# First tiles of pooled attention: which engine sums which piece of k and v, where the gate products stand, and q of the second block in two transfers

## The chip, the core and the metric

The kernel runs on one core of a Trainium2 chip. A core has five engines, each with its own instruction queue: TensorE (PE in the profile, with PEld for its weight loads), VectorE (DVE), ScalarE (ACT), GpSimd (POOL) and SyncE (SP, which here only issues transfers). They meet through semaphores. PE writes its products to PSUM; DVE and ACT read PSUM and SBUF, and POOL works on SBUF. The metric is the device time of one execution in microseconds, the median of several runs.

## The reference, cut to what matters

Eight batches of eight heads with 576 queries each. k and v are averaged over groups of eight rows, so 72 keys are left per head; attention over them is followed by a mixture of eight experts whose routing depends on all tokens.

```python
k_p = k.reshape(B, H, Sp, pool, D).mean(axis=3)
v_p = v.reshape(B, H, Sp, pool, D).mean(axis=3)
scores = scale * np.matmul(q, k_p.transpose(0, 1, 3, 2))
scores = scores - np.max(scores, axis=-1, keepdims=True)
attn = np.exp(scores)
attn = attn / (np.sum(attn, axis=-1, keepdims=True) + 1e-09)
out = np.matmul(attn, v_p)
# x = out by token; logits = x @ w_gate; each token goes to one expert, at most N // E to each
h = np.maximum(x[mask] @ w1[e], 0.0)
out[mask] = h @ w2[e]
```

## The kernel before

**Tiles and blocks.** The 4608 tokens are worked in 36 tiles of 128. A block is one batch: its k (`rawk`, four pairs of heads, each 8 x 72 numbers a partition), its v (`rawv`, five chunks of 8 x 64) and its q (`rawq`). A block has 4.5 tiles, so tile 4 takes queries of blocks 0 and 1 and needs the sums of both. The pooled k stands in `kblk`, the pooled v with a mask in `vblk`; `vblk` also has eight columns that hold v times the gate weights, so that the attention products give the routing's logits too, and one column of ones for the sum of the weights.

**Sums of a block.** `pool_k` (L171) adds eight rows in three steps, 8 to 4 to 2 to 1 (L175, L176, and L179 twice, once for each head of a pair). `pool_v` (L181) does the same for v (L188 to L190) and then multiplies the sums by the mask into `vblk` (L198). For blocks 1 to 7 POOL does all of this, one block behind the other. For block 0 the work is shared: `pool_k` runs on DVE for three of the four pairs, `add_k` (L144) adds the last pair on PE as eight products with the unit matrix, and ACT copies the result (L152). Of v, DVE adds three chunks, `add_v` (L154) adds two on PE, ACT copies and masks these, and POOL masks DVE's.

**Gate columns.** `prep_v` (L202) transposes the sums of v on PE (L211), ACT copies them, `prep_g` (L215) multiplies them by the gate weights on PE (L220), and DVE masks them into `vblk` (L221).

**A tile.** `st_s` (L224) computes the scores into `pss`, which has one buffer. `softmax` (L236) takes the maximum (L240) and the difference (L241) on DVE, which frees `pss`, and the exponential on ACT (L242). One tile later `st_e` transposes the weights (L259) in two parts `pse` and `rt`, and ACT copies them to `eT` (L260). Two tiles later `st_av` makes the attention products into `psa` (L272), and three tiles later `norm` divides on DVE (L284 to L297) and stores.

**What sets the order.** The schedule is written out by hand in `run`: each engine works in the order in which the program emits its instructions, and the loop over tiles interleaves them. `plan` sets at which tile POOL's sums of a block and the loads of a later one are issued. `behind` puts `prep_v` directly behind the scores of the block's first full tile (tile 5 for block 1) and `prep_g` behind the next. For block 0, `prep_v` stands at tile 1's end and `prep_g` ahead of tile 2's scores. SP issues the transfers of block 0 in pieces and then k, v and q of blocks 1 and 2. Before all this PE is kept busy by 13 products of ones (`warm`, L503), and DVE makes constants for the routing (`more`, L464 on).

Of the kernel before, what the change touches and what calls it, by code (L numbers as in the profile page):

```python
# [23 lines left out]
class Attention:  # L24
# [119 lines left out]
    def add_k(self, b, j):  # L144

        nc = self.nc
        ps = self.ps0[:, 0, 384:456]
        for t in range(8):
            nc.tensor.matmul(ps, self.ident, self.rk[b][:, j, t], start=(t == 0), stop=(t == 7))
        for a in range(2):  # L150
            h, y = slice(64 * a, 64 * a + 64), slice(72 * a, 72 * a + 72)
            nc.scalar.activation(self.kblk[b % 4][h, j, y], ps[h], AF.Copy)  # L152

# [27 lines left out]
    def pool_v(self, b, eng, c=slice(0, 5), blocks=None):  # L181
# [9 lines left out]

        for m0, m1 in ((0, 1), (1, 2), (2, 5)):
            m0, m1 = max(m0, c.start), min(m1, c.stop)
            if m0 < m1:
# [3 lines left out]
                (blocks or eng).tensor_tensor(v[:, o, :64].rearrange("p (c i) d -> p c i d", c=n),  # L198
# [16 lines left out]
    def prep_g(self, b):  # L215
# [3 lines left out]
        for n, o in enumerate((slice(0, 40), slice(40, 72), slice(72, 88))):  # L219
            nc.tensor.matmul(ps[:, o], self.vT[:, n], self.wblk[:, o], start=True, stop=True)  # L220
        nc.vector.tensor_tensor(self.vblk[b % 4][:, :, 64:72], ps[:, :88].rearrange("p (n e) -> p n e", e=8),  # L221
                                self.mask[:, :, None].to_broadcast([128, 11, 8]), op=OP.mult)
# [11 lines left out]

    def softmax(self, i):
        nc = self.nc  # L236
        ps = self.pS.pop(i)[:, :, :288].rearrange("p g (h y) -> p g h y", h=4)
        mx = self.wk.tile([128, 2, 4], F32, name="mx")
        e = self.wk.tile([128, 2, 4, 72], F32, name="e", bufs=3)
        nc.vector.tensor_reduce(mx, ps, axis=AX.X, op=OP.max)  # L240
# [86 lines left out]
    def run(self, ctx, full, consts, more, after, end, warm):  # L327
# [82 lines left out]
class Routing:  # L410
# [24 lines left out]
    def consts(self, jp, ident):  # L435
# [25 lines left out]
        self.jp = jp  # L461

    def more(self):
        nc, cst, J, NC, jp = self.nc, self.cst, self.J, self.NC, self.jp  # L464
        self.tri = cst.tile([128, 128], BF, name="tri")
        nc.vector.tensor_scalar(self.tri, jp, 0.0, None, op0=OP.is_gt)
        self.untri = cst.tile([128, 128], BF, name="untri")
        nc.vector.tensor_scalar(self.untri, self.tri, -31.0, None, op0=OP.mult)

# [4 lines left out]
        self.spread = cst.tile([128, 224], F16, name="spread")  # L474
# [1043 lines left out]
```

## Time and profile before

| what | value |
|---|---|
| median of 3 runs (lowest, highest) | 602.14 us (601.81, 602.21) |
| the profiled execution | 602.19 us, its span 600.4 us |
| ACT busy over the span | 306.1 us (51%) |
| POOL busy in 20 to 100 us, by the windows view | 9.47 to 9.71 of each 10 us |
| DMA share in the same view, 10 to 70 us | 1.01 to 1.02 |
| DMA queue of SP, q1 | 70.66 MB, 35.6% of 16 engines over the span |
| granted TensorE clock | 0.984 in the mean, 0.74 in 125 to 150 us |

The page gives busy time over the whole span, which mixes attention (to about 130 us), routing (to about 155 us) and the experts. Where a change touches the first 30 us only, the timeline and the chain of work that ended last, both for that window, say more. In a row of the timeline stand the start, the busy time, the engine, the line of the program, the operation, what it writes and reads with shapes, and in brackets how long the engine was idle before it and what it waited for. In a row of the chain stand the start, the length, the engine, and the tile with the line.

### The profile page before, as it was taken

The page shows a single profiled execution, that of the slowest core. Times are in us where ns is not written, and L with a number is a line of the kernel's source. Part 1 is how long each engine was busy: PE and PEld are TensorE (multiplying, and loading weights), DVE is VectorE, ACT ScalarE, POOL GpSimd, SP SyncE. Part 2 cuts the span into 40 slices and gives each one's busy share as a digit, 9 for nine tenths or more (in the row PEclk, how much of TensorE's full clock was granted, in tenths as well). Part 3 has the DMA queues.
Part 4 walks back from the last instruction along what each step waited for, and adds up shares of the span by engine and source line. Part 5 has one row for each costly group of instructions (what it writes and reads, how often), then busy time and mean ns, then how long its engine had stood idle before and what let it go on. Part 6 is the DMA issues. An engine that isn't in the chain of part 4 may idle for free.

```text
span 600.4 us, 11097 instructions
## 1 busy us (share of the span) xinstructions
PE 576.1 (96%) x4061; PEld 510.1 (85%) x4061; DVE 396.6 (66%) x1155; ACT 306.1 (51%) x629; POOL 176.6 (29%) x219
## 2 busy tenths in 40 slices
PE   8999999995899999999999999999999999999993
PEld 5999999983798789779978987997899899889972
DVE  7677887987886778758965886496477437416200
ACT  7444444451461375385774585276449627835210
POOL 1999999100300410231132112122221211220021
PEclk9999999995999999999999999999999999999998
DMA  8999972122530862548547346543743563450010
GB/s 353 419 422 408 423 292 89 72 89 88 168 142 23 257 202 84 162 109 293 98 107 251 129 98 201 167 106 73 257 135 80 158 228 78 100 192 11 2 58 26
DMA packets 63872, 99.83 MB, mean 166 GB/s; under 512 B 34736, under 2 KB 34752, under 8 KB 61120
## 3 DMA queue, kind: packets, MB, share of 16 engines
q1 hardware_dynamic: 52560, 70.66, 35.6%
q0 software_dynamic: 5920, 18.89, 10.0%
q10 hardware_dynamic: 5328, 9.48, 4.2%
q8 instruction: 34, 0.56, 0.4%
q14 instruction: 30, 0.25, 0.1%
HBM read 72.40 MB, written 18.87 MB: 152 GB/s over the span
## 4 chain that ended last, share of the span: by engine, by line
PE 78%; issue 7%; DVE 6%; POOL 3%; DMA 3%; ACT 1%; POOLq 0%; another core or an unknown queue 0%; SPq 0%; ACTq 0%; DVEq 0%
PE h L1094 30%; PE h L1130 25%; PE psa L272 6%; PE pss L230 5%; PE h L1135 4%; PE pse L259 2%; DMA xg<-xd,rows 1%; PE rt L259 1%; PE rt L503 1%; PE rt L641 1%; DVE e L241 1%; DMA out_dram<-yt,rows 1%; PE rt L604 1%; PE rt L220 1%; POOL out_dram L1110 1%
## 5 line engine op out<-in xcount | busy, mean ns | idle before, releaser
L1130 PE MATMUL h<-w2h,hh 128*128 128x512 f32 x256 | 102.2, 399 | 0.3 <-PEq L1209 0.3
L1130 PE MATMUL h<-w2l,hh 128*128 128x512 f32 x256 | 101.2, 395 | 0.0
L1130 PE MATMUL h<-w2h,hl 128*128 128x512 f32 x256 | 100.9, 394 | 0.0
L1110 POOL DMA_INDIRECT out_dram<-yt,rows x36 | 37.0, 1028 | 205.7 <-ACT yt L1150 180.6
L1099 ACT ACTIVATE hh<-h 128x256 fp32r<-128x256 f32 (+2 forms) x129 | 52.8, 410 | 80.8 <-PE h L1094 80.3
L1094 PE MATMUL h<-xh,w1h 128*128 128x256 f32 (+2 forms) x516 | 93.2, 299 | 0.2 <-ACT xh L1069 0.2
L1094 PE MATMUL h<-xl,w1h 128*128 128x256 f32 (+2 forms) x516 | 92.2, 299 | 0.0
L1094 PE MATMUL h<-xh,w1l 128*128 128x256 f32 (+2 forms) x516 | 91.2, 297 | 0.7 <-DVE w1l L1047 0.7
L1094 PEld LDWEIGHTS h<-xh,w1h 128*128 128x128 f32 x516 | 76.6, 190 | 1.2 <-ACT xh L1069 0.5
L1094 PEld LDWEIGHTS h<-xh,w1l 128*128 128x128 f32 x516 | 76.2, 190 | 1.1 <-DVE w1l L1047 1.1
L1094 PEld LDWEIGHTS h<-xl,w1h 128*128 128x128 f32 x516 | 76.7, 190 | 0.1
L1003 POOL DMA_INDIRECT xa<-xd,rows x33 | 33.4, 1013 | 130.6 <-ACT xg L1021 63.4
L1150 ACT ACTIVATE yt<-h 128x512 f32<-128x512 f32 x32 | 19.1, 598 | 98.7 <-PE h L1130 76.6
L1104 DVE SCALAR_TENSOR_TENSOR hl<-h,hh 128x256 fp32r<-128x256 f32 (+2 forms) x129 | 57.0, 447 | 18.4 <-ACT raw L1102 7.6
L272 PE MATMUL psa<-vblk,eT 128*128 128x146 f32 (+3 forms) x390 | 59.3, 301 | 0.1
L1130 PEld LDWEIGHTS h<-w2l,hh 128*128 128x128 f32 x256 | 48.1, 188 | 9.3
L1130 PEld LDWEIGHTS h<-w2h,hh 128*128 128x128 f32 x256 | 48.4, 189 | 8.9 <-issue 0.7
L1047 DVE TENSOR_TENSOR w1l<-raw,w1h 128x512 fp32r<-128x512 f32 x64 | 41.6, 685 | 21.6 <-ACT w1h L1043 21.6
L1130 PEld LDWEIGHTS h<-w2h,hl 128*128 128x128 f32 x256 | 48.3, 189 | 8.5
L272 PEld LDWEIGHTS psa<-vblk,eT 128*128 128x128 f32 (+1 forms) x390 | 50.8, 179 | 1.5 <-issue 0.3
L1056 DVE TENSOR_TENSOR w2l<-raw,w2h 128x512 fp32r<-128x512 f32 x64 | 43.2, 680 | 2.1 <-ACT w2h L1053 2.0
L230 PE MATMUL pss<-kblk,rawq 128*128 128x144 f32 (+1 forms) x320 | 43.6, 294 | 0.1
(226 smaller groups left out, 948.8 us busy)
## 6 DMA issues: line engine op xcount, KB each, us to landing
raw<-in_moe_w_dram SPq DMA_DIRECT2D x64, 512.0 KB, 5.6
xd<-xt ACTq DMA_DIRECT2D x36, 256.0 KB, 3.1
rawv<-in_v_dram SPq DMA_DIRECT2D x7, 1280.0 KB, 13.7
rawk<-in_k_dram SPq DMA_DIRECT2D x7, 1152.0 KB, 12.5
rawq<-in_q_dram SPq DMA_DIRECT2D x7, 1152.0 KB, 13.8
rawk<-in_k_dram SPq DMA_DIRECT2D x2, 576.0 KB, 3.9
rawv<-in_v_dram SPq DMA_DIRECT2D x1, 768.0 KB, 7.9
rawq<-in_q_dram SPq DMA_DIRECT2D x1, 640.0 KB
```

Of the source, the lines that this page charges most:

```text
L230: nc.tensor.matmul(ps[cols, j // 2, 144 * (j % 2):144 * (j % 2) + 144], self.q_of(b, j, n, cols.stop - cols.start), self.kblk[b % 4][:, j] ...
L272: self.nc.tensor.matmul(o[h], self.eT[i][:, c, h], self.vblk[b % 4][:, self.BLOCKS[c]:self.BLOCKS[c + 1]], start=(c == cs[0]), stop=(c == ...
L1003: self.nc.gpsimd.indirect_dma_start(out=to[:n], out_offset=None, in_=self.xd, in_offset=bass.IndirectOffsetOnAxis(ap=rows[:n, t:t + 1], ax ...
L1047: self.nc.vector.tensor_tensor(l, raw, h.bitcast(F32), op=OP.subtract)
L1056: self.nc.vector.tensor_tensor(self.w2l[:, i], self.raw2[e][:, i], self.w2h[:, i].bitcast(F32), op=OP.subtract)
L1094: nc.tensor.matmul(ps[:, :m], a[:, j, fs], b[:, j, o], start=(n == 0), stop=(n == 11))
L1099: nc.scalar.activation(hh[:, f, o], ps[:, :m], AF.Relu)
L1104: later(0.65, 0.4, lambda f=f, o=o, m=m, ps=ps: nc.vector.scalar_tensor_tensor(hl[:, f, o], ps[:, :m], 0.0, hh[:, f, o].bitcast(F32), op0= ...
L1110: st = nc.gpsimd.indirect_dma_start(out=rows, out_offset=bass.IndirectOffsetOnAxis(ap=idx, axis=0), in_=y, in_offset=None)
L1130: nc.tensor.matmul(ps, a[:, f, o], b[:, f], start=(f == 0 and k == 0), stop=(f == 7 and k == 2))
L1135: nc.tensor.matmul(ps, self.hl[:, f, 512:], b[:, f], start=(f == 0 and k == 0), stop=(f == 7 and k == 1))
L1150: self.nc.scalar.activation(y, ps, AF.Copy)
```

## The change

- The last pair of block 0's k is summed on POOL; `add_k` with its products and copies is gone. DVE's share is as before.
- Of block 0's v, DVE adds two chunks instead of three and POOL adds the third. The masks are a function of their own, `pool_blocks`.
- Of block 1's k, POOL adds three pairs and DVE the last, behind tile 2's softmax.
- The gate products of block 0 stand behind tile 2's scores, and DVE writes the gate columns between the maximum and the difference of that tile; the maximum is a function of its own, `top`. At tile 2 both parts of the transposes stand ahead of the attention products.
- For blocks 1 and 2, `prep_v` stands at the end of the tile's PE work (`after_sums`) instead of directly behind its scores.
- q of block 1 is loaded in two parts, the first (5/9, enough for tiles 4 to 6) ahead of v.
- Seven small constants of the routing (`tri`, `untri`, the zeros of `spread`, two `g`) are made on POOL ahead of its sums instead of on DVE behind its sums.

```diff
-    def add_k(self, b, j):
-        ps = self.ps0[:, 0, 384:456]
-        for t in range(8):
-            nc.tensor.matmul(ps, self.ident, self.rk[b][:, j, t], start=(t == 0), stop=(t == 7))
-        for a in range(2):
-            h, y = slice(64 * a, 64 * a + 64), slice(72 * a, 72 * a + 72)
-            nc.scalar.activation(self.kblk[b % 4][h, j, y], ps[h], AF.Copy)
...
     def pool_k(self, b, eng, halves=(slice(0, 4),)):
-        src = self.rk.pop(b)
-        t1 = self.wk.tile([128, 4, 4, 72], F32, name="tk1", bufs=1)
-        t2 = self.wk.tile([128, 4, 2, 72], F32, name="tk2", bufs=1)
+        src = self.rk[b]
+        if b not in self.tk:
+            self.tk = {b: [self.wk.tile([128, 4, n, 72], F32, name=f"tk{n}", bufs=1) for n in (4, 2)]}
+        t1, t2 = self.tk[b]
...
-    def pool_v(self, b, eng, c=slice(0, 5), blocks=None):
+    def pool_v(self, b, eng, c=slice(0, 5), blocks=True):
...
+        if blocks:
+            self.pool_blocks(b, eng, c)
+
+    def pool_blocks(self, b, eng, c):
...
-        nc.vector.tensor_tensor(self.vblk[b % 4][:, :, 64:72], ps[:, :88].rearrange("p (n e) -> p n e", e=8),
-                                self.mask[:, :, None].to_broadcast([128, 11, 8]), op=OP.mult)
+        def put():
+            nc.vector.tensor_tensor(self.vblk[b % 4][:, :, 64:72], ps[:, :88].rearrange("p (n e) -> p n e", e=8),
+                                    self.mask[:, :, None].to_broadcast([128, 11, 8]), op=OP.mult)
+        return put
...
+    def top(self, i):
+        ps = self.pS[i][:, :, :288].rearrange("p g (h y) -> p g h y", h=4)
+        self.mx = self.wk.tile([128, 2, 4], F32, name="mx")
+        self.nc.vector.tensor_reduce(self.mx, ps, axis=AX.X, op=OP.max)
...
-        for b in (1, 2):
-            self.load_k(b)
-            self.load_v(b)
-            self.load_q(b)
+        n = 4 * self.cut(1)
+        self.load_k(1)
+        self.load_q(1, slice(0, n))
+        self.load_v(1)
+        self.load_q(1, slice(n, 4 * S))
+        self.load_k(2)
+        self.load_v(2)
+        self.load_q(2)
...
-            self.add_k(0, 3)
+            self.pool_k(0, nc.gpsimd, (slice(3, 4),))
             self.pool_k(0, nc.vector, (kh[0], slice(2, 3)))
...
-            plan(first[b - 2] + 1 if b > 2 else b, self.pool_k, b, nc.gpsimd)
+            plan(first[b - 2] + 1 if b > 2 else b, self.pool_k, b, nc.gpsimd, (slice(0, 3 if b == 1 else 4),))
...
-            behind[first[b] + (b == 1)] = lambda b=b: self.prep_v(b)
-            behind[first[b] + 1 + (b == 1)] = lambda b=b: self.prep_g(b)
+            (after_sums if b < 3 else behind)[first[b] + (b == 1)] = lambda b=b: self.prep_v(b)
+            behind[first[b] + 1 + (b == 1)] = lambda b=b: self.prep_g(b)()
...
         for n in range(nt):
+            self.st_s(n)
             if n == 2:
-                self.prep_g(0)
-            self.st_s(n)
+                put = self.prep_g(0)
+                self.top(2)
+                put()
...
-            if n >= 2 and len(self.parts(n - 2)) == 1:
+            if n > 2 and len(self.parts(n - 2)) == 1:
...
+            if n in after_sums:
+                after_sums[n]()
+            if n != 2:
+                self.top(n)
             self.softmax(n)
             if n == 0:
                 self.put_v(0, vh[1])
-                self.pool_v(0, nc.vector, vh[0], blocks=nc.gpsimd)
+                self.pool_v(0, nc.vector, slice(0, 2), blocks=False)
+                self.pool_v(0, nc.gpsimd, slice(2, 3), blocks=False)
+                self.pool_blocks(0, nc.gpsimd, vh[0])
+            if n == 2:
+                self.pool_k(1, nc.vector, (slice(3, 4),))
...
+        nc.gpsimd.tensor_scalar(self.tri, jp, 0.0, None, op0=OP.is_gt)
...
+        nc.gpsimd.tensor_scalar(self.untri, self.tri, -31.0, None, op0=OP.mult)
...
+        nc.gpsimd.memset(self.spread, 0.0)
...
+            nc.gpsimd.memset(g, 0.0)
+            nc.gpsimd.memset(g[J:J + 1], -1.0 - EDGE)
```

Lines of the changed kernel are numbered anew (L175 becomes L166, L188 becomes L180, L230 becomes L231). POOL's first work on data in the kernel before, behind its sixteen little fills: the masks of block 0's v, then block 1's k.

```order
L86 MEMSET edges 128x1 x16
L198 TENSOR_TENSOR vblk_177<-vsum,mask 128x2x64
L198 TENSOR_TENSOR vblk_177<-vsum,mask 128x3x64
L198 TENSOR_TENSOR vblk_177<-vsum,mask 128x2x64
L175 TENSOR_TENSOR tk_316<-rawk 128x1152
L176 TENSOR_TENSOR tk_317<-tk_316 128x576
L179 TENSOR_TENSOR kblk_131<-tk_317 64x4x72 x2
```

The same place of POOL's queue in the changed kernel, behind the fills and the constants: the last pair of block 0's k, one chunk of its v, the masks, and then block 1's k.

```order
L166 TENSOR_TENSOR tk_224<-rawk 128x288
L167 TENSOR_TENSOR tk_225<-tk_224 128x144
L170 TENSOR_TENSOR kblk_131<-tk_225 64x72 x2
L180 TENSOR_TENSOR tv_279<-rawv 128x256
L181 TENSOR_TENSOR tv_280<-tv_279 128x128
L182 TENSOR_TENSOR vsum<-tv_280 128x64
L195 TENSOR_TENSOR vblk_178<-vsum,mask 128x2x64
L195 TENSOR_TENSOR vblk_178<-vsum,mask 128x3x64
L195 TENSOR_TENSOR vblk_178<-vsum,mask 128x2x64
L166 TENSOR_TENSOR tk_314<-rawk 128x864
L167 TENSOR_TENSOR tk_315<-tk_314 128x432
L170 TENSOR_TENSOR kblk_132<-tk_315 64x3x72 x2
```

Two groups of sums of block 0 stand ahead of the masks now, and block 1's k has 864 elements instead of 1152.

DVE from the difference of tile 1 to the maximum of tile 3 and what follows, before (`pss` are the scores, `vblk` with `psa,mask` the gate columns):

```order
L241 TENSOR_TENSOR e<-pss,mx 128x576
L221 TENSOR_TENSOR vblk_177<-psa,mask 128x11x8
L240 TENSOR_REDUCE mx<-pss 128x8
L241 TENSOR_TENSOR e<-pss,mx 128x576
L240 TENSOR_REDUCE mx<-pss 128x8
L241 TENSOR_TENSOR e<-pss,mx 128x576
L284 RECIPROCAL rinv<-psa 128x8
```

And in the changed kernel:

```order
L245 TENSOR_TENSOR e<-pss,mx 128x576
L239 TENSOR_REDUCE mx<-pss 128x8
L220 TENSOR_TENSOR vblk_178<-psa,mask 128x11x8
L245 TENSOR_TENSOR e<-pss,mx 128x576
L166 TENSOR_TENSOR tk_314<-rawk 128x288
L167 TENSOR_TENSOR tk_315<-tk_314 128x144
L170 TENSOR_TENSOR kblk_132<-tk_315 64x72 x2
L239 TENSOR_REDUCE mx<-pss 128x8
L245 TENSOR_TENSOR e<-pss,mx 128x576
L288 RECIPROCAL rinv<-psa 128x8
```

The gate columns moved behind the maximum of tile 2, and the sums of block 1's last k pair stand ahead of the maximum of tile 3.

PE from the transposes of block 0's v sums to tile 3's scores, before (`rt` and `pse` are the transposes of the weights, `psa` with `vblk` the attention products):

```order
L211 MATMUL psa<-ident,vsum 128x128 x3
L220 MATMUL psa<-wblk,vT 128x40
L220 MATMUL psa<-wblk,vT 128x32
L220 MATMUL psa<-wblk,vT 128x16
L230 MATMUL pss<-kblk_130,rawq 128x144 x4
L259 MATMUL pse<-ident,e 127x128 x3
L272 MATMUL psa<-vblk_177,eT_171 128x2x73
L272 MATMUL psa<-vblk_177,eT_171 128x3x73
L272 MATMUL psa<-vblk_177,eT_171 128x2x73
L259 MATMUL rt<-ident,e 127x128 x2
L272 MATMUL psa<-vblk_177,eT_171 128x2x73 x2
L230 MATMUL pss<-kblk_130,rawq 128x144 x4
```

And in the changed kernel:

```order
L208 MATMUL psa<-ident,vsum 128x128 x3
L231 MATMUL pss<-kblk_131,rawq 128x144 x4
L217 MATMUL psa<-wblk,vT 128x40
L217 MATMUL psa<-wblk,vT 128x32
L217 MATMUL psa<-wblk,vT 128x16
L263 MATMUL pse<-ident,e 127x128 x3
L263 MATMUL rt<-ident,e 127x128 x2
L276 MATMUL psa<-vblk_178,eT_172 128x2x73
L276 MATMUL psa<-vblk_178,eT_172 128x3x73
L276 MATMUL psa<-vblk_178,eT_172 128x2x73 x3
L231 MATMUL pss<-kblk_131,rawq 128x144 x4
```

Tile 2's scores moved ahead of the gate products, and the second part of the transposes moved ahead of the attention products.

More of the change, by code (lines that the diff above doesn't have):

```diff
@@ L184, in pool_v @@
             self.sums[b] = self.wk.tile([128, 5, 64], F32, name="vsum")
-        t1 = self.wk.tile([128, 5, 256], F32, name="t1", bufs=1)
-        t2 = self.wk.tile([128, 5, 128], F32, name="t2", bufs=1)
-        s, v, B = self.sums[b], self.vblk[b % 4], self.BLOCKS
+        if b not in self.tv:
+            self.tv = {b: [self.wk.tile([128, 5, n], F32, name=f"tv{n}", bufs=1) for n in (256, 128)]}
+        t1, t2 = self.tv[b]
+        s = self.sums[b]
         eng.tensor_tensor(t1[:, c], src[:, c, :256], src[:, c, 256:], op=OP.add)
@@ L190, in pool_v @@
         eng.tensor_tensor(s[:, c], t2[:, c, :64], t2[:, c, 64:], op=OP.add)
+        if blocks:
+            self.pool_blocks(b, eng, c)
+    def pool_blocks(self, b, eng, c):
+        s, v, B = self.sums[b], self.vblk[b % 4], self.BLOCKS
         for m0, m1 in ((0, 1), (1, 2), (2, 5)):
@@ L197, in pool_v @@
                 k = (B[m1] - B[m0]) // n
-                (blocks or eng).tensor_tensor(v[:, o, :64].rearrange("p (c i) d -> p c i d", c=n),
+                eng.tensor_tensor(v[:, o, :64].rearrange("p (c i) d -> p c i d", c=n),
                                   s[:, m0:m1, None, :].to_broadcast([128, n, k, 64]),
@@ L233, in st_s @@
         self.pS[i] = ps
+    def top(self, i):
+        ps = self.pS[i][:, :, :288].rearrange("p g (h y) -> p g h y", h=4)
+        self.mx = self.wk.tile([128, 2, 4], F32, name="mx")
+        self.nc.vector.tensor_reduce(self.mx, ps, axis=AX.X, op=OP.max)
     def softmax(self, i):
         nc = self.nc
-        ps = self.pS.pop(i)[:, :, :288].rearrange("p g (h y) -> p g h y", h=4)
-        mx = self.wk.tile([128, 2, 4], F32, name="mx")
+        ps, mx = self.pS.pop(i)[:, :, :288].rearrange("p g (h y) -> p g h y", h=4), self.mx
         e = self.wk.tile([128, 2, 4, 72], F32, name="e", bufs=3)
-        nc.vector.tensor_reduce(mx, ps, axis=AX.X, op=OP.max)
         nc.vector.tensor_tensor(e, ps, mx[:, :, :, None].to_broadcast([128, 2, 4, 72]), op=OP.subtract)
@@ L334, in run @@
         self.rk, self.rv, self.sums, self.qT = {}, {}, {}, {}
+        self.tk, self.tv = {}, {}
         self.pS, self.e, self.eT, self.pA = {}, {}, {}, {}
@@ L337, in run @@
         first = [S * b // 128 for b in range(B)]
-        at, behind = {}, {}
+        at, behind, after_sums = {}, {}, {}
         def plan(i, f, *a):
@@ L461, in consts @@
         self.jp = jp
+        self.tri = cst.tile([128, 128], BF, name="tri")
+        nc.gpsimd.tensor_scalar(self.tri, jp, 0.0, None, op0=OP.is_gt)
+        self.untri = cst.tile([128, 128], BF, name="untri")
+        nc.gpsimd.tensor_scalar(self.untri, self.tri, -31.0, None, op0=OP.mult)
+        self.spread = cst.tile([128, 224], F16, name="spread")
+        nc.gpsimd.memset(self.spread, 0.0)
+        self.gs = [cst.tile([128, 16], BF, name=f"g{i}") for i in range(2)]
+        for g in self.gs:
+            nc.gpsimd.memset(g, 0.0)
+            nc.gpsimd.memset(g[J:J + 1], -1.0 - EDGE)
     def more(self):
         nc, cst, J, NC, jp = self.nc, self.cst, self.J, self.NC, self.jp
[L465 to L468, printed above, removed]
         t = cst.tile([128, 4], I32, name="td")
@@ L473, in more @@
         nc.vector.tensor_scalar(self.diag, t[:, None, :].to_broadcast([128, 20, 4]), 0.0, None, op0=OP.is_equal)
-        self.spread = cst.tile([128, 224], F16, name="spread")
-        nc.vector.memset(self.spread, 0.0)
         with nc.allow_low_precision(reason="0 and 1"):
@@ L482, in more @@
         nc.scalar.activation(self.blk[:, 18:], self.i36[:, 17:19, None].to_broadcast([128, 2, NC]), AF.Copy)
-        self.gs = [cst.tile([128, 16], BF, name=f"g{i}") for i in range(2)]
-        for g in self.gs:
-            nc.vector.memset(g, 0.0)
-            nc.vector.memset(g[J:J + 1], -1.0 - EDGE)
         self.q16 = cst.tile([128, NC], F16, name="q16a")
```

1 line of the change is left out of this document (removed).

## The prediction

> **What bounds the kernel now.** I read the page first, then the chain of work that ended last, then the timeline of the first 30 us engine by engine, because the change touches nothing later. The page says that TensorE (PE) is the bound over the whole span:
>
> ```profile
> PE 576.1 (96%) x4061; PEld 510.1 (85%) x4061; DVE 396.6 (66%) x1155; ACT 306.1 (51%) x629; POOL 176.6 (29%) x219
> ```
>
> An average of 96% hides the start, where PE waits. The chain of the first 60 us shows who is waited for:
>
> ```profile
> 1.98 5.66 PE rt L503 x13
> 7.64 1.74 PE psa L149 x16
> 9.38 1.14 PE pss L230 x8
> ...
> 10.55 0.77 DVE mx L240
> 11.34 0.76 DVE e L241
> ...
> 14.03 1.23 POOL vblk L198 x3
> 15.26 2.58 POOL tk L175
> ...
> 26.65 0.55 PE rt L211 x3
> 27.20 0.33 PE pse L259 x3
> 27.53 0.87 PE psa L272 x6
> 28.40 0.22 PE rt L259 x2
> 28.62 0.50 PE psa L272 x4
> 29.13 0.98 PE pss L230 x8
> 30.11 0.57 PE rt L220 x6
> ```
>
> The columns are start, length and the work. Three stretches follow each other: PE's warming products and the sums of the k piece (to 9.38), DVE's softmax and v sums (to 14.0), and GpSimd (POOL) summing block 1 without a pause until 26.6. From there PE is the chain, and the rows give what each part of a tile costs PE: scores 0.98 to 1.21 (I take 1.10), transposes 0.33 and 0.22, attention products 0.87 and 0.50, together 3.02 us a tile; gate products 0.57. A tile's time below is the start of its scores.
>
> ```profile
> 15.88 1.23 PE L230 MATMUL pss<-kblk,rawq 128*128 128x144 f32 x8
> 18.87 1.19 PE L230 MATMUL pss<-kblk,rawq 128*128 128x144 f32 x8
> 21.91 1.20 PE L230 MATMUL pss<-kblk,rawq 128*64 128x144 f32 x16
> 25.07 1.14 PE L230 MATMUL pss<-kblk,rawq 128*128 128x144 f32 x8
> 28.96 1.14 PE L230 MATMUL pss<-kblk,rawq 128*128 128x144 f32 x8
> ```
>
> These are tiles 2 to 6. All tiles behind tile 6, the routing and the experts hang on each other, so a shift of tile 6 should reach the end whole.
>
> **The change, part by part.** The sums are carried by these rows of DVE and POOL:
>
> ```profile
> 1.87 0.58 POOL L86 MEMSET edges<- 128x1 f32 x16
> 6.58 0.46 DVE L175 TENSOR_TENSOR tk<-rawk 128x288 f32<-128x288 f32 x1
> 7.08 0.31 DVE L176 TENSOR_TENSOR tk<-tk 128x144 f32<-128x144 f32 x1
> 7.42 0.47 DVE L179 TENSOR_TENSOR kblk<-tk 64x72 f32<-64x72 f32 x2
> 12.01 0.95 DVE L188 TENSOR_TENSOR t<-rawv 128x768 f32<-128x768 f32 x1
> 13.59 0.36 DVE L190 TENSOR_TENSOR vsum<-t 128x192 f32<-128x192 f32 x1
> 16.14 0.25 DVE L221 TENSOR_TENSOR vblk<-psa,mask 128x88 f32<-128x88 f32 x1 [0.73 <-ACT e L242]
> 15.22 2.62 POOL L175 TENSOR_TENSOR tk<-rawk 128x1152 f32<-128x1152 f32 x1
> 21.12 2.91 POOL L188 TENSOR_TENSOR t<-rawv 128x1280 f32<-128x1280 f32 x1
> 25.74 0.86 POOL L190 TENSOR_TENSOR vsum<-t 128x320 f32<-128x320 f32 x1
> ```
>
> A straight line through the POOL rows is 0.19 us + 2.12 ns an element; through the DVE rows 0.16 us + 1.03 ns. Gaps between them are 0.07 and 0.03 us.
>
> *Head.* The 16 sum products (1.74) and ACT's two copies go. POOL sums the piece instead: 288, 144 and twice 72 elements are 0.80 + 0.50 + 0.68, with gaps 2.2 us. Its data has landed by 6.58, when DVE starts on the same transfer, so it is done by 8.8. PE is free at 7.64, does three quarters of tile 0's scores by 8.5 and the last by 9.1; before, they ended at 10.52. **Gain 1.4.** The moved constants cost DVE 0.9 us of rows; POOL does them between 2.45, when it now falls idle, and 6.58. No row shows such an operation on POOL. From below the cost is nothing; at twice DVE's, as the slopes of 2.12 and 1.03 ns stand, it is about 1.8 us, which the gap covers, and I take that. Past 4.1 us every further microsecond delays tile 0, up to the whole 1.4.
>
> *Tiles 1 and 2.* DVE's softmax of tile 0 ends at 9.13 + 0.77 + 0.03 + 0.76 = 10.7. The v sums shrink to two parts of three: 512, 256 and 128 elements are 0.69 + 0.43 + 0.29, with gaps 1.5 us, to 12.2 (before 13.95). PE has done the v products and tile 1's scores by 12.1. Softmax of tile 1 takes 1.55, so tile 2 starts at 13.8, **2.1 earlier**. POOL's third part (0.73 + 0.46 + 0.33) ends at 12.3 and the block products (1.23) at 13.6, before block 1's k lands.
>
> *Gate products behind the third scores.* Before, they ran while PE waited for DVE; now they are on the path: 13.8 + 1.10 + 0.57 + 0.33 + 0.22 = 16.0. DVE's maximum of tile 2 (15.0 to 15.8) and the gate columns (0.25) end at 16.05, then the attention products (1.37): tile 3 at 17.45, so **0.7 is given back** and 1.4 is left.
>
> *Block 1's last k piece on DVE, q in two parts.* The three DVE rows at 6.58 to 7.42 say 1.24 us, with gaps 1.3: 16.9 to 18.2. The maximum of tile 3 queues behind it on DVE and cannot start before 17.45 + 1.2 = 18.7, so 0.5 is to spare; if the cover goes, each lost microsecond delays tile 4 by as much. For the transfers, these are block 1's three issues in the timeline, and behind them what the DMA view answers for single issues: size and us to landing, block 0's large v piece first, issued by 2.7, then block 1's k, v and q.
>
> ```profile
> 3.76 0.43 SPq L121 DMA_DIRECT2D rawk<-in_k_dram  x1
> 4.23 0.50 SPq L126 DMA_DIRECT2D rawv<-in_v_dram  x1
> 4.78 0.45 SPq L136 DMA_DIRECT2D rawq<-in_q_dram  x1
> ...
> rawv<-in_v_dram SPq DMA_DIRECT2D x1, 768.0 KB, 7.9
> ...
> rawk<-in_k_dram SPq DMA_DIRECT2D x1, 1152.0 KB, 11.3
> ...
> rawv<-in_v_dram SPq DMA_DIRECT2D x1, 1280.0 KB, 13.9
> ...
> rawq<-in_q_dram SPq DMA_DIRECT2D x1, 1152.0 KB, 16.7
> ```
>
> Issue plus time to landing: block 0's v by 10.6, just ahead of DVE's 10.7; block 1's k at 15.1, v at 18.1, q at 21.5. The queue is full throughout, so 640 KB of q ahead of v take half of the 3.1 us that v took: the first q part lands at 16.7, v at 19.7, the rest near 21.4. Without the split, tile 4 could not start before 21.5 and 1.0 us would be lost; with it the limits are PE (17.45 + 3.02 = 20.47), DVE (20.25) and POOL, whose three quarters of k (2.02 + 1.11 + 2 x 0.65 and gaps, 4.6 us from 15.1) end at 19.7. **Tile 4 at 20.5, tile 5 at 23.55.** The second q part is wanted first by tile 7.
>
> *The transposes of v's sums at the end of tile 5.* Before, PE stood behind tile 5's scores (25.07 + about 1.05) until POOL's sums at 26.6: 0.5 us. Now they come at 23.55 + 3.02 = 26.6, and POOL has the sums at 19.75 + 2.91 + 1.55 (the line, for 640 elements) + 0.86 + gaps = 25.2. With 0.33 for them, tile 6 starts at 26.9 instead of 28.96. **Sum: 1.4 + 0.5 + roundings = 2.1 us.**
>
> *Downstream.* POOL is ahead by 1.4 us only, and block 3's sums meet PE next:
>
> ```profile
> 51.93 0.86 POOL L190 TENSOR_TENSOR vsum<-t 128x320 f32<-128x320 f32 x1
> ...
> 53.61 0.55 PE L211 MATMUL rt<-ident,vsum 128*128 128x128 f32 x3
> ```
>
> That is 0.8 us to spare, 0.1 after the shifts. So a gain above 2.2 would be cut there, and 2.1 just passes. The profiled execution took 602.19 us (span 600.4); 602.19 - 2.1 = **600.1**. The median of 602.14 is 0.05 from it, which changes nothing at this precision.
>
> **The rivals.**
>
> *DVE and POOL take turns (slower).* In the trace before, DVE never adds two tensors from SBUF while POOL adds: its last such sum ends at 13.95 and POOL's first operation on data starts at 14.03. The rows where both are busy have DVE reading PSUM, and neither is slowed: the maxima of all 36 tiles lie between 682 and 759 ns.
>
> ```profile
> L240 DVE TENSOR_REDUCE mx<-pss x36: 682/756/759, 10.5 to 127.3; 128x8 f32<-128x576 f32 x36
> ```
>
> The change lets the two add side by side in three places, so the trace neither supports nor excludes that one blocks the other. If each operation holds the other up until it is done, in turn: in the head POOL's 2.0 and DVE's last 1.55 us run one after the other from 6.2, tile 0 ends near 10.3, and tile 3 is back at 18.9. Then DVE's four sums of block 1 (0.46, 0.31, 0.24, 0.24), ready at 18.4, alternate with POOL's 0.65, 0.65 and the 2.91 of v: the last ends at 23.9, the softmax of tile 3 at 25.45, tile 4 starts 3.5 late, and less the 0.5 of the stall the time is **605.2**. What decides is whether POOL's 2.91 gets in before DVE's last sum.
> [...]
>
> *They block each other, but DVE keeps its turn.* If DVE's sums follow each other without POOL in between, they run from 18.3 to 19.6, tile 4 starts at 21.95 as before, and only the stall of 0.5 is gained: **601.6**; with one POOL operation of 0.65 between each, about 1 us more: 602.6.
>
> *A new wait at block 3, or constants too long on POOL.* Either leaves a gain of about 1.3: **600.9**.
>
> **How the numbers follow.** Forecast 0.48, taking turns 0.20, blocked but mild 0.20, smaller gain 0.10, something else 0.02 (slower). Of this kernel a measurement tells 0.2% (1.2 us) from no change: faster 0.58, within 0.2% 0.20, slower 0.22. The forecast alone spans 599.4 to 600.7 (2.8 off if DVE and PE lose less than I count and POOL has more to spare at block 3, 1.5 if that meeting bites). The range goes to the mild cases, 599.4 to 602.8; the rival of 605.2 is left out with its 0.2.
>
> **What would show it.** Right: no products ahead of tile 0's scores, its maximum starting near 9.1; tile 2 near 13.8, tile 4 near 20.5, tile 6 near 26.9; no wait of PE for POOL's v sums. Wrong: DVE's or POOL's sums at 6 to 9, 11 to 13 or 17 to 20 us taking longer than their sizes say, a maximum of tile 3 later than 19, POOL still on constants at 6.6, or PE waiting for POOL at tile 13.

## The result, and the profile after

The changed kernel takes **606.7 us** in the median of 4 runs (605.41 to 607.08), the kernel before 602.07 us (4 runs, 601.81 to 602.21): the ratio is 1.0072, with a 95% interval of 1.0058 to 1.0087. It is slower by 0.7%. The forecast of 600.1 us and its range of 599.4 to 602.8 missed it. The profiled execution took 606.40 us (span 604.6), 4.2 us more than the one before, and is 0.3 us from the median.

The page's row of the engines and the maxima of all tiles on DVE (shortest, median and longest in ns) read nearly as before; neither shows the loss:

```profile
PE 575.4 (95%) x4045; PEld 509.3 (84%) x4045; DVE 402.0 (66%) x1152; ACT 305.7 (51%) x627; POOL 180.9 (30%) x233
```

```profile
L239 DVE TENSOR_REDUCE mx<-pss x36: 684/757/759, 9.7 to 131.6; 128x8 f32<-128x576 f32 x36
```

PE is busy 0.7 us less in a span that is 4.2 us longer, so PE stood still for 4.9 us more; part of its busy time is slow besides. The maxima have one input, from PSUM, and take at most 759 ns although POOL sums beside them, as in the profile before (682 to 759). The starts of the tiles' scores say where the time went. "Forecast" is the prediction's own working.

| tile | before | forecast | after | what the step to it adds to after minus forecast |
|---|---|---|---|---|
| 2 | 15.88 | 13.8 | 14.43 | 0.63 |
| 3 | 18.87 | 17.45 | 18.20 | 0.12 |
| 4 | 21.91 | 20.5 | 24.46 | 3.21 |
| 5 | 25.07 | 23.55 | 29.33 | 1.82 |
| 6 | 28.96 | 26.9 | 32.88 | 0.20 |

Together 6.0 of the 6.3 us between 600.1 and 606.4. Two steps carry 5.0 of them: from tile 3 to 4, and from tile 4 to 5. These are the rows of the timeline for tiles 2 to 6 after:

```profile
14.43 1.22 PE L231 MATMUL pss<-kblk,rawq 128*128 128x144 f32 x8 [0.90 <-PE psa L208]
...
18.20 1.14 PE L231 MATMUL pss<-kblk,rawq 128*128 128x144 f32 x8
...
24.46 1.52 PE L231 MATMUL pss<-kblk,rawq 128*64 128x144 f32 x16 [3.20 <-DVE rinv L288]
...
29.33 1.14 PE L231 MATMUL pss<-kblk,rawq 128*128 128x144 f32 x8
...
32.88 1.15 PE L231 MATMUL pss<-kblk,rawq 128*128 128x144 f32 x8
```

PE stands still for 3.20 us ahead of tile 4. The reciprocal that the row names (`rinv`) only stood last on VectorE; the work ahead of it is in the chain of the work that ended last (start, length, engine, tile and line):

```profile
17.27 1.22 DVE tk L166
...
18.58 0.58 DVE tk L167
19.18 0.59 DVE kblk L170
19.78 2.96 DVE kblk L170
...
22.77 0.77 DVE mx L239
23.56 0.76 DVE e L245
...
24.46 1.52 PE pss L231 x15
25.98 0.94 PE pse L263 x3
26.92 1.71 PE psa L276 x6
```

Block 1's last k piece on DVE runs from 17.18 to 22.73, and not 1.3 us long as forecast. The last addition of 72 elements, 0.24 us in the profile before, stands there with 2.96 us. The maximum of tile 3 comes at 22.77 and not at 18.7. What POOL does at that time, by the timeline:

```profile
18.24 1.44 POOL L170 TENSOR_TENSOR kblk<-tk 64x216 f32<-64x216 f32 x2
19.76 2.89 POOL L180 TENSOR_TENSOR tv<-rawv 128x1280 f32<-128x1280 f32 x1
```

POOL's first v sum runs from 19.76 to 22.65, and DVE's addition from 19.78 to 22.73: it starts when the other starts and ends when it has ended. The three additions ahead of it, beside POOL's sums of k, are longer too: 1.22, 0.58 and 0.59 us in the chain, 0.46, 0.31 and 0.24 in the profile before.

The second step shows in the chain too: behind the hole tile 4's transposes take 0.94 us (0.33 before) and the first attention products 1.71 (0.87). The windows view gives the granted clock of PE in the last columns but two, behind the busy times of the five engines:

```profile
22.00:24.00 2.00, 0.00 (x0) 0.00 (x0) 1.93 (x3) 0.00 (x0) 1.92 (x2) 1.00 0.96 390
24.00:26.00 2.00, 1.54 (x17) 1.19 (x17) 1.25 (x4) 0.68 (x1) 1.84 (x4) 0.85 1.01 423
26.00:28.00 2.00, 2.00 (x8) 1.94 (x9) 1.84 (x5) 0.49 (x1) 2.00 (x3) 0.50 1.03 432
28.00:30.00 2.00, 2.00 (x15) 2.00 (x14) 0.61 (x2) 0.91 (x2) 1.92 (x2) 0.80 0.98 406
```

The clock falls to 0.50 behind the hole. In windows of 0.2 us it is 1.00 up to 25.2 us, 0.50 from 25.4 to 28.6 and 1.00 again from 28.8, so by the means of 0.85, 0.50 and 0.80 it was half for 0.6 + 2.0 + 0.8 = 3.4 us. Tile 4 therefore takes 4.87 us instead of the 3.16 before.

And the head, where POOL and DVE add side by side, by the timeline of both:

```profile
5.95 1.23 DVE L170 TENSOR_TENSOR kblk<-tk 64x144 f32<-64x144 f32 x2
7.22 0.69 DVE L166 TENSOR_TENSOR tk<-rawk 128x288 f32<-128x288 f32 x1
...
9.67 0.76 DVE L239 TENSOR_REDUCE mx<-pss 128x8 f32<-128x576 f32 x1 [0.22 <-PE pss L231]
```

```profile
6.22 0.79 POOL L166 TENSOR_TENSOR tk<-rawk 128x288 f32<-128x288 f32 x1 [1.55 <-DMA rawk<-in_k_dram]
7.10 0.49 POOL L167 TENSOR_TENSOR tk<-tk 128x144 f32<-128x144 f32 x1
7.67 0.82 POOL L170 TENSOR_TENSOR kblk<-tk 64x72 f32<-64x72 f32 x2
```

DVE's pair of additions into `kblk` takes 1.23 instead of 0.62 us and its next sum 0.69 instead of 0.46. POOL's first two sums last what the line through its rows said, its last pair 0.82 instead of 0.68. The maximum of tile 0 comes at 9.67: 0.9 earlier than before, not 1.4.

### The profile page after: what moved, and what is told of

Same layout as the page of the kernel before. It is cut to its first block, busy times and chain, and to the rows that moved or that the text cites. A ratio compares the mean times of both kernels' runs of the same rounds, so it can differ in the third digit from the quotient of the medians.

```text
span 604.6 us, 11083 instructions
## 1 busy us (share of the span) xinstructions
PE 575.4 (95%) x4045; PEld 509.3 (84%) x4045; DVE 402.0 (66%) x1152; ACT 305.7 (51%) x627; POOL 180.9 (30%) x233
## 3 DMA queue, kind: packets, MB, share of 16 engines
HBM read 72.40 MB, written 18.87 MB: 151 GB/s over the span
## 4 chain that ended last, share of the span: by engine, by line
PE 80%; DVE 7%; issue 7%; DMA 2%; POOL 1%; ACT 1%; POOLq 0%; another core or an unknown queue 0%; SPq 0%; ACTq 0%; DVEq 0%
PE h L1112 30%; PE h L1148 26%; PE psa L276 6%; PE pss L231 6%; PE h L1153 4%; PE pse L263 2%; PE rt L263 1%; DVE kblk L170 1%; PE rt L659 1%; DVE e L245 1%; PE rt L622 1%; PE rt L217 1%; DMA out_dram<-yt,rows 1%; DMA raw<-in_moe_w_dram 1%; PE tp L1085 1%
## 5 line engine op out<-in xcount | busy, mean ns | idle before, releaser
L231 PE MATMUL pss<-kblk,rawq 128*128 128x144 f32 (+1 forms) x320 | 44.0, 295 | 6.0 <-DVE rinv L288 3.2
L231 PEld LDWEIGHTS pss<-kblk,rawq 128*128 128x128 f32 (+1 forms) x320 | 37.2, 179 | 9.8 <-issue 4.5
```

The lines of the kernel that those rows point to most:

```text
L231: nc.tensor.matmul(ps[cols, j // 2, 144 * (j % 2):144 * (j % 2) + 144], self.q_of(b, j, n, cols.stop - cols.start), self.kblk[b % 4][:, j] ...
```

## The experiments

Theory, from the profile after: an addition on DVE with two inputs from SBUF is held as long as an instruction of POOL that started ahead of it runs (**held**: 2.96 us instead of 0.24, beside POOL's 2.89), and the hole that this makes halves PE's clock (**clock**: 0.50 behind the 3.20 us). Rivals: DVE waits for a semaphore of POOL's, since both use the tiles `tk`; or the new order itself costs the time. All edits are against the changed kernel where nothing else is said. The first four experiments ran on one chip, the others on a second one; on both the kernel before takes 602.8 to 602.9 us (medians of 21 runs).

**All of block 1's k on POOL.**

```diff
-            plan(first[b - 2] + 1 if b > 2 else b, self.pool_k, b, nc.gpsimd, (slice(0, 3 if b == 1 else 4),))
+            plan(first[b - 2] + 1 if b > 2 else b, self.pool_k, b, nc.gpsimd, (slice(0, 4),))
...
-            if n == 2:
-                self.pool_k(1, nc.vector, (slice(3, 4),))
```

> The changed kernel with block 1's k summed by POOL alone, as before; DVE's four sums behind tile 2 are gone. Theory (DVE's sums of two SBUF tensors are held until POOL's running operation is done): the hole of 3.2 us ahead of tile 4 goes; POOL ends the sums at 14.95 + 5.9 = 20.8, PE is free at 18.2 + 3.0 = 21.2, so tile 4 starts at 21.2 (21.91 before, 24.46 in the changed kernel) and tile 6 near 27.6; the time is 600.5 to 601.2. Rival (the loss is made in the head, between 6 and 13 us): the time stays near 606.

Measured: 602.85 us (11 runs, 602.51 to 604.34), ratio to before 1.0005 (0.9996 to 1.0014). From tile 3 to 4 it takes 3.00 us, from 4 to 5 3.16, and tile 6 starts at 28.67. Handing that one piece to DVE is the whole loss: the new order is still in this kernel, and the loss is gone. The rest of the change is worth nothing here that can be measured. The expected 600.5 to 601.2 us was missed: tile 2 starts at 15.20 on this chip (14.43 in the profile after), and tile 6 1.1 us later than expected.

**The same piece on DVE by one-input reductions.**

```diff
-                self.pool_k(1, nc.vector, (slice(3, 4),))
+                for a in range(2):
+                    h, y = slice(64 * a, 64 * a + 64), slice(72 * a, 72 * a + 72)
+                    nc.vector.tensor_reduce(self.kblk[1][h, 3, y], self.rk[1][h, 3].rearrange("p t y -> p y t"),
+                                            axis=AX.X, op=OP.add)
```

> The changed kernel, but DVE sums block 1's last k pair with two reductions over the eight rows, each reading one SBUF tensor, in place of four additions of two. Theory: they aren't held, take 0.75 to 1.2 us each although POOL works beside them, the maximum of tile 3 starts at 19.6 at the latest, tile 4 near 21.3, the time is 600.3 to 601.2. Rival (DVE is held whatever it reads from SBUF, or by the transfers): the two together take over 4 us, and the time stays over 604.

Measured: 602.91 us (11 runs, 602.21 to 604.15), ratio 1.0004 (0.9995 to 1.0013). DVE's and POOL's rows in the timeline:

```profile
19.18 2.42 DVE L414 TENSOR_REDUCE kblk<-rawk 64x72 f32<-64x576 f32 x2
```

```profile
18.93 1.34 POOL L170 TENSOR_TENSOR kblk<-tk 64x216 f32<-64x216 f32 x2
20.39 2.90 POOL L180 TENSOR_TENSOR tv<-rawv 128x1280 f32<-128x1280 f32 x1
```

The reductions read more (2 x 576 elements a partition) and still end after 2.42 us, at 21.60, beside the same POOL instruction that held the addition for 2.96 and that runs to 23.29 here. So it is the form of the DVE instruction that made the difference, as **held** says.

**Tiles of its own for DVE's piece**, so that DVE and POOL share no buffer for their partial sums (both still write `kblk`).

```diff
-                self.pool_k(1, nc.vector, (slice(3, 4),))
+                d1, d2 = (self.wk.tile([128, m, 72], F32, name=f"tkd{m}", bufs=1) for m in (4, 2))
+                s = self.rk[1][:, 3]
+                nc.vector.tensor_tensor(d1, s[:, :4], s[:, 4:], op=OP.add)
+                nc.vector.tensor_tensor(d2, d1[:, :2], d1[:, 2:], op=OP.add)
...
+                    nc.vector.tensor_tensor(self.kblk[1][h, 3, y], d2[h, 0], d2[h, 1], op=OP.add)
```

> The changed kernel, but DVE's sums of block 1's k use tiles of their own, so that they have no semaphore of POOL to wait for (in the changed kernel the first two wait for one). Theory: nothing changes, the four sums still take over 5 us together, 606 +- 0.7. Rival (DVE waits for POOL through the shared tiles): the sums take 1.3 us, and the time is near 601.

Measured: 607.15 us (4 runs, 606.92 to 608.83), ratio 1.0079 (1.0064 to 1.0095).

```profile
20.12 3.54 DVE L418 TENSOR_TENSOR kblk<-tkd 64x72 f32<-64x72 f32 x2
```

```profile
20.69 2.89 POOL L180 TENSOR_TENSOR tv<-rawv 128x1280 f32<-128x1280 f32 x1
```

DVE's last addition ends at 23.66, POOL's sum at 23.58. The loss is all there without the shared tiles `tk`, and the reductions above write the same `kblk` without being held: the semaphore falls. PE's hole is 2.52 us here, and the clock is halved behind it too (0.50 in 26 to 28 us).

**PE kept busy in the hole** by 14 products of ones behind tile 3.

```diff
             for f in (*e, *av):
                 f()
+            if n == 3:
+                warm(14)
```

> The changed kernel with 14 products of ones (about 3.0 us at full clock) on PE behind tile 3, in the hole ahead of tile 4. They add no wait: DVE is what tile 4 waits for. Theory with the clock: tile 4 starts at 24.5 as in the changed kernel, but tile 5 follows it by 3.1 us, not 4.9, and the time is 1.5 to 1.8 us below the changed kernel's, near 604.7. Rival (the slow products behind the hole aren't the idle time's doing): no change, 606.4.

Measured: 606.99 us (4 runs, 605.43 to 607.24), ratio 1.0061 (1.0045 to 1.0076).

```profile
23.42 3.18 PE L523 MATMUL rt<-ones 128*128 128x512 bf16 x14
26.91 1.27 PE L231 MATMUL pss<-kblk,rawq 128*64 128x144 f32 x16 [0.31 <-DVE e L245]
...
30.14 1.14 PE L231 MATMUL pss<-kblk,rawq 128*128 128x144 f32 x8
```

Tile 4 now takes 3.23 us instead of 4.87, at a granted clock of 1.00 from 24 to 30 us, so the 1.6 us behind the hole are the clock's. The total of the profiled execution (607.24) hardly shows it, because in it the clock was halved somewhere else: from 10.5 to 13.9 us (0.61 in 10 to 12 us, 0.53 in 12 to 14), which put tile 1 at 13.69 (12.17 in the first experiment). The other three executions have no profile; none reached the expected 604.7. In the profiles of the two runs above it was halved in the head as well (0.51 in 10 to 12 us in both). PE's granted clock from 10 to 12 us, in the windows of the run with reductions, where it was halved, and of the first experiment, where it was not:

```profile
10.00:12.00 2.00, 2.00 (x11) 2.00 (x10) 1.57 (x3) 0.00 (x0) 0.63 (x1) 0.51 1.07 439
```

```profile
10.00:12.00 2.00, 2.00 (x20) 2.00 (x18) 1.75 (x5) 0.00 (x0) 0.57 (x1) 1.00 1.06 432
```

With the sum products gone, PE waits twice in the head (0.98 us for q and 0.65 us for DVE in the first of these profiles, 0.80 and 0.65 in the second). In some executions the clock is halved behind such waits and in some not: behind 1.11 and 0.65 us in the profile after it is 1.00 from 10 to 14 us, and behind 1.45 and 0.65 in the changed kernel on the second chip the 16 products of v take 1.95 us, as in the profile after (3.44 in the run with reductions).

**The kernel before, profiled on the second chip**, without an edit.

> The kernel before itself, unchanged, profiled on the chip of the experiments, where it takes 602.81 us (median of 21 runs) and where transfers land about 0.8 us later than in the profiles of before and after. It gives the tile starts and the clock against which the experiments are read. Expected if everything in the head follows the transfers: tile 0 near 9.9, tile 6 near 29.6, half clock in the head nowhere. If the transfers of q and v are not what this kernel's head waits for: tile 0 at 9.2 to 9.4 and tile 6 near 29.0, and the late landing costs only the kernels that sum the first k piece on GpSimd.

Measured: 602.84 us, tile 0 at 8.94, tile 6 at 29.69. DVE's first sum waits for its transfer until 5.65, a microsecond longer than in the profile before (4.65), and yet the maximum of tile 0 stands at 10.55 in both. It is the later block that pays: POOL starts on block 1's k at 15.92 instead of 15.22, and PE waits 0.72 us for its v sums instead of 0.44. So neither expectation came true whole: tile 6 is where the first had it, tile 0 earlier than both. Tile 4 pays too, 3.58 us instead of 3.16, because its weight loads pause:

```profile
21.92 0.19 PEld L230 LDWEIGHTS pss<-kblk,rawq 128*64 128x64 f32 x2
22.36 0.93 PEld L230 LDWEIGHTS pss<-kblk,rawq 128*64 128x64 f32 x14 [0.24 <-issue]
```

The profile doesn't name what they wait for. It fits q of block 1, which by the prediction landed at 21.5 in the profile before and would land near 22.2 here if it is as late as block 1's k; with q in two parts tile 4 takes 3.16 us (first experiment, and products back below). No run has the split alone.

**Reductions, and PE kept busy in the head** (against the kernel with reductions).

```diff
-        warm(13)
+        self.warm = warm
+        warm(18)
...
+            if i == 0 and j == 1:
+                self.warm(3)
```

> The changed kernel with block 1's last k piece on VectorE by two one-input reductions (as in the run before of that name), and PE kept busy in the head: 18 warming products instead of 13, and 3 more between the two halves of tile 0's scores, where PE waited 0.65 us. [...] Rival (the clock of the head is chance and not PE's idle time, or the products delay the scores): some executions still lose 1.5 us, median 602.9 as without the products.

Measured: 602.52 us (11 runs, 602.23 to 602.93), ratio 0.9994 (0.9985 to 1.0003). Without the additional products 5 of 11 runs lay at 603.5 to 604.2 and 6 at 602.2 to 602.9; with them all 11 lie under 603. The spread of 1.3 us is gone, as it should be if idle PE costs the clock in the head, and the one of the five that was profiled (603.70) had the half clock there (0.51 in 10 to 12 us). In the profile with the additional products no wait is shown ahead of either half of tile 0's scores, and the 16 products of v take 1.95 us instead of 3.44. The other four have no profile, and the two kernels ran on different chips: that idle PE cost them the same is likely, but not shown. The median is above the 600.9 to 602.0 that the author estimated with idle PE as the cause: tile 2 starts at 15.21 and tile 6 at 28.92, since from tile 2 on PE works without a pause, and the head did not become shorter.

**The sum products back on PE** (against the first experiment: `add_k` as before in place of POOL's piece).

```diff
-            self.pool_k(0, nc.gpsimd, (slice(3, 4),))
+            self.add_k(0, 3)
```

> The changed kernel with both shifts of k between POOL and its neighbours undone: the first block's last piece on PE and ACT (add_k) as before, and the whole of block 1's k on POOL. What is left of the change is the order (gate products, transposes of v's sums at the tile's end), q in two parts, v in thirds and the constants on POOL. Theory (the k sums on DVE and POOL are the whole loss; the order is worth the 0.5 us stall ahead of tile 6): no hole, clock full in the head, tile 6 at 28.2 to 28.7 in the profile, median 602.0 to 602.5 against 602.8, spread as small as before's (0.5 us). Rival (the order itself costs something, the gate products on the path): tile 6 at 29 or later, median 602.8 or more.

Measured: 602.73 us (11 runs, 602.3 to 602.98), ratio 0.9998 (0.9989 to 1.0007). This prices the head. The same two DVE instructions, first with POOL summing beside them (first experiment), then without:

```profile
6.75 1.24 DVE L170 TENSOR_TENSOR kblk<-tk 64x144 f32<-64x144 f32 x2
8.02 0.69 DVE L166 TENSOR_TENSOR tk<-rawk 128x288 f32<-128x288 f32 x1
```

```profile
6.58 0.62 DVE L180 TENSOR_TENSOR kblk<-tk 64x144 f32<-64x144 f32 x2
7.23 0.46 DVE L176 TENSOR_TENSOR tk<-rawk 128x288 f32<-128x288 f32 x1
```

DVE's six sums take 4.16 us there (5.46 to 9.62) and 3.24 here (5.29 to 8.53). With the products on PE, tile 0 starts later (8.86 against 8.29) but tile 2 no later (15.06 against 15.20, with the first transfer 0.17 us earlier): with the transfers as they land here, taking the products away from PE gains nothing. Against the kernel before as profiled on this chip, tile 5 takes 3.55 us instead of 4.18, so the move of the transposes of v's sums does take the stall away; tile 4 gives another 0.42. But the 1.16 us at tile 6 come out as 0.96 at tile 35 and 0.1 in the median.

**One more DVE instruction in each of tiles 14 to 33 of the kernel before**, its result unused: a two-input sum in even tiles, a one-input reduction in odd ones.

```diff
...
+            if 14 <= n < 34:
+                y = self.wk.tile([128, 384], F32, name=f"probe{2 - n % 2}", bufs=1)
+                if n % 2:
+                    nc.vector.tensor_reduce(y, self.pr[:, :, None], axis=AX.X, op=OP.add)
+                else:
+                    nc.vector.tensor_tensor(y, self.pr, self.pr, op=OP.add)
```

> The kernel before with one more VectorE instruction on 384 elements in each of tiles 14 to 33, its result unused: in even tiles a sum of two tensors from SBUF (probe2), in odd tiles a reduction with one input (probe1). The line through VectorE's rows gives 0.56 us for the sum alone. [...] Rival (both slow each other evenly, by bandwidth): probe2 is lengthened by a constant factor under 2 and probe1 too.

Measured: 611.47 us. By **held** the sum should take the 0.56 us of DVE's line where POOL is idle, and up to about 3.5 us where POOL sums (its own 0.56 and POOL's longest sum of 2.9), and the reduction the same everywhere. The groups by line (count, shortest, median and longest in ns), then single rows of the timeline of DVE and of POOL:

```profile
L404 DVE TENSOR_TENSOR probe<-probe x10: 549/772/2723, 61.5 to 129.4; 128x384 f32<-128x384 f32 x10
L402 DVE TENSOR_REDUCE probe<-probe x10: 542/542/545, 66.6 to 132.7; 128x384 f32<-128x384 f32 x10
```

```profile
61.46 2.72 DVE L404 TENSOR_TENSOR probe<-probe 128x384 f32<-128x384 f32 x1
...
77.99 1.27 DVE L404 TENSOR_TENSOR probe<-probe 128x384 f32<-128x384 f32 x1
...
99.23 0.55 DVE L404 TENSOR_TENSOR probe<-probe 128x384 f32<-128x384 f32 x1
```

```profile
60.87 2.91 POOL L188 TENSOR_TENSOR t<-rawv 128x1280 f32<-128x1280 f32 x1
...
77.31 1.54 POOL L189 TENSOR_TENSOR t<-t 128x640 f32<-128x640 f32 x1
78.92 1.06 POOL L190 TENSOR_TENSOR vsum<-t 128x320 f32<-128x320 f32 x1
...
99.38 1.91 POOL L179 TENSOR_TENSOR kblk<-tk 64x288 f32<-64x288 f32 x2
```

The reduction takes 542 to 545 ns whatever POOL does. The sum takes 0.55 us where POOL is idle (the last three of the ten). In six cases it starts 0.2 us or more ahead of the end of an instruction of POOL, and there it ends 0.40 to 0.42 us after that one's end (64.18 against 63.78, 79.26 against 78.85). POOL's next instruction is held by the sum in turn (1.06 us instead of 0.86 for 320 elements). The sum at 99.23 starts in the last 0.1 us of a POOL instruction: it is not lengthened, and POOL's next pair pays (1.91 us instead of 1.65). So in these rows the two do not share a rate: the POOL instruction that the sum meets keeps its usual length (2.91 us at 60.87, 1.54 at 77.31), and the sum takes up to 2.72 us instead of 0.55.

**The changed kernel on the second chip**, without an edit.

> The changed kernel itself, unchanged, timed on the chip of the experiments, so that each of them can be set against it there. Expected: 606.9 to 607.2 us as its variants with the sum of block 1's last k piece on VectorE (607.15 and 606.99), tile 3 near 18.9, tile 4 near 25.2, and the clock halved for 3.4 us behind the hole; 605.5 to 606.5 only if the two variants cost something themselves.

Measured: 607.36 us (5 runs, 607.26 to 609.07), ratio 1.0084 (1.007 to 1.0098). Tile 0's maximum stands at 10.53, against 10.55 of the kernel before on the same chip: with the transfers landing later there is nothing left of the gain at tile 0. Tile 2 starts at 15.26 against 15.89, mostly since the gate products no longer stand ahead of it (put back in the next run, they cost 0.5 there); tile 3 starts at 19.03, tile 4 at 25.32, tile 5 at 30.19.

**The gate products back ahead of tile 2's scores**, in the kernel with reductions and more warming.

```diff
+            if n == 2:
+                self.prep_g(0)()
             self.st_s(n)
-            if n == 2:
-                put = self.prep_g(0)
-                self.top(2)
-                put()
...
-            if n > 2 and len(self.parts(n - 2)) == 1:
+            if n >= 2 and len(self.parts(n - 2)) == 1:
```

> The kernel of the reductions and more warming, with the gate products of block 0 put back ahead of tile 2's scores, the gate columns ahead of its maximum, and the attention products between the two parts of the transposes as before. Theory (PE waits 0.89 us ahead of tile 2's scores anyway, for the VectorE that frees their buffer; behind the scores the 0.57 us of gate products are on the path): tile 2 starts 0.2 to 0.4 us later than 15.21, tile 3 at 18.5 to 18.65 instead of 18.98, tile 6 0.3 to 0.45 us earlier than 28.92, median 602.0 to 602.3 against 602.52 without. Rival (tile 2 waits for the copy of the transposed sums by more than it gains): tile 3 at 18.95 or later, no gain.

Measured: 603.16 us (11 runs, 602.61 to 603.49), ratio 1.0003 (0.9994 to 1.0012). Tile 3 starts at 18.70 instead of 18.98, near the expected 18.5 to 18.65. But then it catches up with DVE's piece:

```profile
22.60 1.29 PE L231 MATMUL pss<-kblk,rawq 128*64 128x144 f32 x16 [0.79 <-DVE rinv L290]
```

The reductions end at 20.87, the maximum of tile 3 queues behind them, PE waits 0.79 us ahead of tile 4, and 0.5 us is lost at tile 6: the median is 0.6 us above that without the move, and not 0.2 to 0.5 below.

**The same move with the products on PE and all of block 1's k on POOL.**

> The same move of the gate products in the kernel with the sum products back on PE and all of block 1's k on POOL: what is left of the change is q in two parts, the transposes of v's sums at the tile's end, v in thirds and the constants. Theory: tile 3 0.3 to 0.45 us earlier than 18.82, but tile 4 waits for POOL's sums of k, which end near 21.3, so tile 6 only 0 to 0.3 earlier than 28.53, median 602.4 to 602.7. Rival (order is worth nothing here): 602.73 as without.

Measured: 602.46 us (11 runs, 602.14 to 602.92), ratio 0.9993 (0.9984 to 1.0002). Tile 6 starts at 28.47 against 28.53 without the move, and tile 3 only 0.12 us earlier, with a first transfer that landed 0.3 us later in this profile (5.61 against 5.29). This is the fastest version by its median, 0.4 us under the kernel before, but its interval includes 1: no version was shown to beat the kernel before.

## Why the prediction was wrong, point by point

**The step that failed** is "the three DVE rows at 6.58 to 7.42 say 1.24 us, with gaps 1.3" with its "0.5 is to spare". Those rows are DVE alone; in the changed kernel POOL sums beside it, and the piece took 5.55 us. The cover of 0.5 us was gone, and by the prediction's own words each lost microsecond delays tile 4: 3.2 us. The prediction had said that the trace before holds no case of both adding, gave both ends, and took the lower one as the likeliest. All four additions were held, the last one for 2.7 us. The kernel with reductions, the one with tiles of its own and the probe show the cause: the hold by POOL's running instruction (2.96 us against 0.24), which the reductions with one input do not meet (542 to 545 ns in the probe, with POOL summing or idle).

**The rival that came true** was "DVE and POOL take turns" at 605.2: POOL's 2.89 us did get in ahead of DVE's last addition, which was its deciding point. It put that addition's end at 23.9 (measured 22.73) and tile 3 at 18.9 (18.20), so it was dearer than the trace there. Its head did not come out (tile 0's scores end at 9.63, not near 10.3); what it lacked was the clock behind the hole, 1.8 us.

**The clock** stands in no step of the prediction. The 3.20 us in which PE stood still cost 1.7 us more (4.87 against 3.16), and the experiment with products in the hole gave 1.6 of it back at tile 5. In the profiles the clock falls to 0.50 behind holes of 3.20 us (after) and 2.52 us (tiles of its own) and to 0.51 in the head of the kernel with reductions, behind two waits of 0.98 and 0.65 us with products between them; behind waits of 1.45 and 0.65 us in the changed kernel on the second chip the 16 products of v took 1.95 us and not 3.44. What decides between the two cases, no run shows.

**Head, 1.4.** The mechanism was right and the size wrong: 0.9 in the profile after, because POOL's sums held DVE's by 0.92 us (first experiment against products back), and 0.0 at tile 0 where the transfers land later. The removed products also left PE idle; some executions of the kernels without added warming were 1.3 us longer, the profiled one of them with a clock of 0.51 from 10 to 12 us. **Constants on POOL:** 1.8 taken, 2.25 measured (2.42 to 4.67), hidden as said.

**Gate products, 0.7 given back.** Tile 2 to 3 takes 3.77 us instead of 2.99: 0.8, right. But PE still waits 0.90 us ahead of tile 2's scores, where the products had stood for nothing; put back there, tile 3 comes 0.28 earlier in the kernel with reductions, and 0.12 with the products on PE.

**q in two parts.** Not tested by the changed kernel: tile 4 waits for DVE there and comes too late to need the split. What the profiles on the second chip say for it is the 0.42 us at tile 4. **Stall at the transposes of v's sums.** Right: POOL's v sums end at 25.2 as worked out. That the changed kernel doesn't wait for them proves little, since its PE is 4 us late; but the versions whose PE is on time (first experiment, products back) don't wait either, and tile 5 to 6 is 3.55 us in all kernels with the move. At the tile's end they cost 0.2 more than counted, though, and again at block 2 (tile 9 takes 3.62 us with products back, 3.31 before); that they wait there for ACT to free `rt` fits the rows (ACT's copy out of it ends at 32.38 in the profile after, the transposes start at 32.52), but was not tried.

**Downstream.** Tile 6 is 3.92 us late and the end 4.2: the shift went through whole. The meeting at block 3 was never reached, since PE is late.

**What stays open:** the two versions with the products back on PE have tile 35 0.95 us earlier than the kernel before, and only 0.1 to 0.4 us less time. In their profiles, the stretch of half clock around the routing (0.50 from 141 to 149 us in the profile before) ends 27.7 and 28.0 us behind tile 35's start, and 24.9 in the kernel before. Over all profiles, the time from tile 35's start to the end of the span is 474.2 to 474.5 us where the stretch ends 24.9 to 26.8 us behind, and 474.4, 474.7, 474.9 and 475.1 where it ends at 27.6, 27.7, 27.9 and 28.0. So a late end of that stretch goes with the loss; nothing here moves it by itself, so this is no test.

## What to carry to other kernels

Before a piece of work moves to DVE or POOL, look at what the other one does at that time: here an addition of two SBUF tensors on DVE, with 72 elements and 0.24 us of its own, lasted 2.96 us beside a POOL sum of 2.89. The rows here show two ways out: a form with one SBUF input (542 to 545 ns with POOL summing or idle), or keeping the two apart in time (0.55 us for a sum of 384 with POOL idle). A duration read from a row where the neighbour was idle was only the lower end here, where the neighbour was busy. And a hole in PE's work can cost twice: here its 3.20 us, and 1.7 us for the half clock behind it, so work that is taken away from PE may have to be replaced by something.

## What the hardware showed that was not expected

- A held DVE instruction is shown as busy: 2.96 us of "busy" for 72 elements, and nothing in the waits says so. The sign is an end that follows closely on the end of a POOL row (23.66 and 23.58, 64.18 and 63.78).
- A held sum ends behind POOL by about what its elements cost on the prediction's line (1.03 ns each): 0.40 us for 384 elements, 0.08 for 72. POOL's next instruction behind a sum of 384 is then 0.2 us longer than alone (1.06 against 0.86), so the delay goes both ways.
- The kernel with reductions was 1.3 us longer in 5 of 11 runs, and in none of 11, on another chip, once PE was kept busy in the head. The one of the five that was profiled had its clock halved from 10.0 to 13.4 us (0.51 in 10 to 12 us, 0.64 in 12 to 14).
- The first transfer of k landed at least 0.6 to 1.0 us later in all profiles on the two chips of the experiments than in those of before and after (DVE's first sum at 5.29 to 5.65 against 4.65 and 4.66). The kernel before does not feel it at tile 2 (15.89 against 15.88); the changed kernel does (15.26 against 14.43).
